# The last 24 visits of a gated attention-and-mixer kernel: score banks, one token block moved, a last sum in two halves

## The chip, the cores and the metric

The kernel runs on one core of a Trainium2 chip. The metric is device time in microseconds (us). The kernel before takes 1671.52 us in the median of three runs (1671.33 to 1672.03). The engines are TensorE (PE; its weight loads are listed as PEld), VectorE (DVE), ScalarE (ACT), GpSimd (POOL) and SyncE (SP), which here only issues DMAs.

## The reference

`x` has 2048 tokens of 640 features. Two branches are mixed by a gate for each token:

```python
g = sigmoid((x * gate_w).sum(-1, keepdims=True))
# branch A: 32 query heads of 20 features share one key and one value head
q = (x @ wq), k = x @ wk, v = x @ wv
p = softmax(q k^T * 20 ** -0.5)
a = (p v, heads side by side) @ wo
# branch B: an MLP over the token axis, 2048 -> 1728 -> 2048
b = (w2 gelu(w1 layernorm(x)^T + b1) + b2)^T
out = g * a + (1 - g) * b
```

All is float32. Products that go through the faster float32r format are split into a high and a low part, and three products (high x high, low x high, high x low) are summed; so each such step has three matmuls.

## The kernel before, in words

**Units and visits.** Attention is cut into 32 units: four blocks of 512 queries times eight groups of four heads. A unit has 16 visits, one for each block of 128 keys, 512 visits in all. A visit has four score matmuls (`qk`, L657; two use rows 0 to 63 of the array, two use rows 64 to 127, so that a pair runs side by side on the two row halves), four exponentials on ScalarE (L660) that turn a score bank in PSUM into a tile `p`, and eight matmuls of `p` with V (`pv_mm`, L684) into the bank `o`. The maximum that the softmax subtracts is found one unit ahead by other score matmuls and a reduction on DVE (L479, L482), stored (`store_max`) and fetched as two extra rows of the queries (`fetch_max`). After the last visit of a unit a chain of steps in `later` (turn, scale, back, high, low, L699 to L728) transposes `o`, divides by the sum, transposes back and splits into `oh` and `ol`, which go to `o_scr` in DRAM.

**Stretches.** Everything else is filled in beside the visits. `ph` lists 326 stretches; each is a set of fill matmuls on one row half, run beside score and maximum matmuls on the other, and carries one or two visits in turn (488 in all). The fill is first the mixer's first product, then its second (`b2_jobs`: one of 16 token blocks for each `st`, in ten stretches when `st < FIVE` and in twelve otherwise, ending on ScalarE at L758, result to `y_scr`), then the product with `wo` for the first `NA` token blocks (`a_jobs`: four stretches each, two results at L888, output at L892). `FIVE` is worked out from `NA` so that there are 326 stretches.

**The tail.** The last 24 visits run in twelve blocks of two (`for n in BLOCKS`, L1072). There are no maxima any more. Each block issues eight score matmuls, four a half, always one visit ahead of the V matmuls (`ends`, L1073; the first block issues nine, the last four), mixes them with fill matmuls of the remaining token blocks (`tail_take`, `tail_job`, L831, an accumulator for each half and each half of the 640 output features, taken up by DVE at L838), and ends with the V matmuls of two visits. Constants X_US, F_US and EXP_US spread the scores over the fill when the program is written; on the chip the order is fixed and TensorE's queue is strictly in order. PSUM has eight banks: three for maxima and fill (`ps_m`), one for fill (`ps_g`), three for scores (`ps_s`) and `o`. The last four token blocks (12 to 15) need heads of the last unit, so their product with `wo` is parted by rows of `wo`: rows 0 to 383 and 384 to 559 as fill, rows 560 to 639 last. For blocks 12 and 13 the middle part is held until after the last visit (L1115); then the last part follows for all four (L1130), DVE, ScalarE and POOL add the parts (L1133, L1136, L1137), and eight output pieces of 128 x 320 go out on the queues of SP and ScalarE (L1142).

**Loads.** `tail_load` brings the transposed heads of a token block and its `y_scr` rows from DRAM into rooms of two large tiles; the first six loads are issued from the last stretches, the rest after visit 502, all on SP.

Of the kernel before, what the change touches and what calls it, by code (L numbers as in the profile page):

```python
# [17 lines left out]
P = 128  # L18
# [14 lines left out]
NA = 10  # L33
# [6 lines left out]
def mix_kernel(ctx: ExitStack, tc: tile.TileContext, A_x, A_wq, A_wk, A_wv, A_wo,  # L40
# [595 lines left out]
    turn_p = [0]  # L636

# [12 lines left out]
    def qk(u, pr, b):  # L650
        n, kb = units[u]
        assert n in back_in
        if kb == 4 and pr == 0 and b == 0:
            new_q(n + 1)
        q = qtiles[n]
        s = ps_s.tile([P, NB], F32, name="s") if spare[0] else next_bank()
        nc.tensor.matmul(s, kst[64 * b:64 * b + 62, kb * P:(kb + 1) * P], q[64 * b:64 * b + 62, pr, :],  # L657
                         start=True, stop=True)
        p = next_p()
        nc.scalar.activation(p, s, AF.Exp, scale=SCALE)  # L660
        ptiles[u, 2 * pr + b] = p
# [12 lines left out]
    osplit = []  # L674
# [3 lines left out]
    def pv_mm(u):  # L678
# [7 lines left out]
        if kb == NS - 1:  # L686
# [27 lines left out]
            def high():  # L714
                osplit[:] = [oh, ol]
                if n < NU - 1:
                    nc.gpsimd.tensor_copy(oh, on)
                else:
                    nc.scalar.activation(oh, on, AF.Copy)

            def low():
                (nc.vector if n == NU - 1 else nc.gpsimd).tensor_sub(ol, on, f32(oh))
                for j, t in enumerate((oh, ol) if n < NU - 1 else ()):
# [70 lines left out]
    CUT = 3 * P  # L794
# [3 lines left out]
    held = (NS - 4, NS - 3)  # L798

    def room(i):  # L800
        t, at = (u0, slot[0])[i % 8 // 4], 3 * D * (i % 4)
        return (t[:, at:at + 2 * D].rearrange("p (j c q) -> p j c q", j=2, q=P), f32(t[:, at + 2 * D:at + 3 * D]))

    def tail_load(i):
        if i < len(jobs):
            st, r0, r1 = jobs[i]
            cols = slice(st * P, (st + 1) * P)
            oT, yt = room(i)
            c0, c1 = r0 // P, r1 // P
            for j in range(2):  # L810
                nc.sync.dma_start(out=f32(oT[:, j, c0:c1]),
                                  in_=o_scr[j, r0:c1 * P, cols].rearrange("(c p) s -> p c s", p=P))
                if r1 > c1 * P:
                    nc.sync.dma_start(out=f32(oT[:r1 - c1 * P, j, c1]), in_=o_scr[j, c1 * P:r1, cols])
            if r0 == 0:
                nc.sync.dma_start(out=yt, in_=y_scr[cols, :])
            loaded.append(i)

    def tail_job(n):
# [5 lines left out]
        def mm(c, k, d, h, first, last):  # L825
            if first:
                acc[d, h] = (ps_g.tile([P, NB], F32, name="g") if h and not d
                             else ps_m.tile([P, NB], F32, name="ms"))
# [3 lines left out]
            if last:  # L832
                sl = slice(d * HD2, (d + 1) * HD2)
# [166 lines left out]
    for i, (st, r0, _) in enumerate(jobs):  # L1000
        if not (r0 and st in held):
            tail_job(i)
# [68 lines left out]

    for n in BLOCKS:  # L1072
# [28 lines left out]
        waiting = {j for h in range(2) for j, _ in tail[h]}  # L1101
        while len(loaded) < len(jobs) and len(loaded) - 8 not in waiting and v >= 501:
            tail_load(len(loaded))
    accs = {}

    for c in range(CUT // P, DC):
        r = min(P, HEAD - c * P)
        for st in held:
            oT, _ = room(len(jobs) - 4 + st - (NS - 4))
            for d in range(2):  # L1110
                if (st, d) not in accs:
                    accs[st, d] = (ps_g.tile([P, NB], F32, name="g") if (st, d) == (held[1], 1)
                                   else ps_m.tile([P, NB], F32, name="ms"))
                for k, (j, w) in enumerate(((0, wo_hi), (1, wo_hi), (0, wo_lo))):
                    nc.tensor.matmul(accs[st, d][:, :HD2], oT[:r, j, c, :], w[:r, c, d * HD2:(d + 1) * HD2],  # L1115
                                     start=(k == 0 and c == CUT // P), stop=False)
    assert not tail[0] and not tail[1]
    for _, f in later[1:]:
        f()
    oh, ol = osplit  # L1120
    ends = {}
    for i in range(4):
        st = NS - 4 + i
        for d in range(2):
            at = pp_pool.tile([P, NB], F32, name="p")
            sl = slice(d * HD2, (d + 1) * HD2)
            acc = accs.get((st, d)) or (ps_s.tile([P, NB], F32, name="s") if (i, d) != (3, 1)
                                        else ps_m.tile([P, NB], F32, name="ms"))
            for k, (o, w) in enumerate(((oh, w_last[0]), (ol, w_last[0]), (oh, w_last[1]))):
                nc.tensor.matmul(acc[:, :HD2], o[:, i * P:(i + 1) * P], w[:, sl],  # L1130
                                 start=(k == 0 and (st, d) not in accs), stop=(k == 2))
            if (i, d) in ((0, 0), (1, 0), (2, 1), (3, 0), (3, 1)):
# [6 lines left out]
    for q, order in ((nc.sync, ((0, 0), (1, 0), (0, 1), (2, 1), (1, 1), (2, 0))), (nc.scalar, ((3, 0), (3, 1)))):  # L1139
# [24 lines left out]
```

## Time and profile before

| | us |
|---|---|
| median of three runs | 1671.52 |
| the profiled execution | 1671.47 |
| its span, first to last instruction | 1669.7 |
| granted TensorE clock | 1.000 |

A page of the profile gives the busy time of each engine. The timeline gives one line for a run of like instructions: start and length in us from the start of the span, the engine, the line in the kernel, output and inputs, shapes, how many, and in brackets the idle time before it with the instruction that ended it. The windows view gives, for a stretch of time, its length, then busy time and number of instructions of PE, PEld, DVE, ACT and POOL, the granted clock, the busy share of the DMA engines and GB/s. A group line with a source line gives shortest/median/longest duration in ns and the first and last start. Matmuls overlap in these records: one lasts longer than the distance to the next. The chain of work that ended last is given on the page as 95% PE, 2% issue and 1% DVE over the whole span; in the last 40 us the view puts it down to issue, and there the timelines of the engines are read instead.

### The profile page before, as it was taken

To read this page: it belongs to the slowest core of one execution; us is meant where nothing else is said; L and a number is where in the kernel's file an instruction comes from. 1 tells how busy PE (TensorE), PEld (TensorE's weight loads), DVE (VectorE), ACT (ScalarE), POOL (GpSimd) and SP (SyncE) were. 2 spreads that over 40 slices of the span, in tenths; PEclk is the share of its full clock that TensorE was granted. 3 is DMA by queue.
4 is the path that set the end of the run, shared out by engine and by line. 5 is a ranking of instruction groups with operands and counts; after the bars stand their busy time and mean duration, and the time that the engine had idled before them with its cause. 6 is when DMAs were issued, how large, how long until landed. Compare 5 with 4: busy or idle time off the path is not lost.

```text
span 1669.7 us, 38827 instructions
## 1 busy us (share of the span) xinstructions
PE 1661.0 (99%) x14865; PEld 1105.5 (66%) x14865; DVE 1435.7 (86%) x2732; ACT 1188.0 (71%) x2346; POOL 606.3 (36%) x759
## 2 busy tenths in 40 slices
PE   9999999999999999999999999999999999999998
PEld 7899666666666666666666666666666566666665
DVE  6689899999989999988888988988888998988933
ACT  4434777777777777777777777777777777777775
POOL 6578555455455554422232332122122220111210
PEclk9999999999999999999999999999999999999999
DMA  7665222222132232222222222212222121333611
GB/s 211 205 176 137 79 71 69 78 58 78 53 84 73 71 82 74 58 60 62 66 75 74 55 62 66 61 52 71 63 66 60 55 65 41 96 111 113 189 51 39
DMA packets 178305, 138.20 MB, mean 83 GB/s; under 512 B 33306, under 2 KB 144055, under 8 KB 178119
## 3 DMA queue, kind: packets, MB, share of 16 engines
q1 hardware_dynamic: 177830, 135.39, 28.9%
q8 instruction: 117, 1.92, 0.5%
q14 instruction: 70, 0.57, 0.1%
q10 hardware_dynamic: 288, 0.33, 0.1%
HBM read 102.36 MB, written 31.65 MB: 80 GB/s over the span
## 4 chain that ended last, share of the span: by engine, by line
PE 95%; issue 2%; DVE 1%; SPq 1%; ACT 0%; DMA 0%; POOL 0%; POOLq 0%; DVEq 0%; ACTq 0%
PE o L684 28%; PE ms L479 18%; PE s L657 13%; PE g L750 10%; PE g L929 7%; PE ms L657 5%; PE pp L298 4%; PE s L479 3%; PE pu L586 3%; PE g L875 2%; DVE mp L482 1%; PE ms L831 0%; ACT p L660 0%; PE pt L290 0%; SPq L195 0%
## 5 line engine op out<-in xcount | busy, mean ns | idle before, releaser
L482 DVE TENSOR_REDUCE mp<-ms 128x1 f32<-128x512 f32 x1514 | 967.2, 685 | 130.2 <-PE ms L479 102.7
L660 ACT ACTIVATE p<-s 128x512 f32<-128x512 f32 x1512 | 820.6, 606 | 299.4 <-PE s L657 280.2
L479 PE MATMUL ms<-kst,qmx 60*128 60x512 f32 x1514 | 646.5, 433 | 1.7 <-DVE mp L482 1.7
L657 PE MATMUL s<-qst,kst 62*128 62x512 f32 x1512 | 601.6, 403 | 0.0
L684 PE MATMUL o<-p,v_sb 128*32 128x512 f32 x4096 | 511.3, 601 | 0.0
L479 PEld LDWEIGHTS ms<-kst,qmx 60*128 60x128 f32 x1514 | 279.0, 184 | 244.9 <-ACT p L660 114.7
L482 DVE TENSOR_REDUCE mp<-s 128x1 f32<-128x512 f32 x534 | 355.6, 683 | 12.0 <-PE s L479 11.8
L660 ACT ACTIVATE p<-ms 128x512 f32<-128x512 f32 x536 | 305.1, 599 | 56.8 <-PE ms L657 50.2
L657 PEld LDWEIGHTS s<-qst,kst 62*128 62x128 f32 x1512 | 278.5, 186 | 55.2 <-DVE flag L670 31.0
L929 PE MATMUL g<-slot,wh 64*128 64x320 f32 x1280 | 297.5, 311 | 0.0
L129 POOL TENSOR_TENSOR wl<-wr,wh 128x512 fp32r<-128x512 f32 x176 | 228.6, 1300 | 43.8 <-PE g L750 17.3
L479 PE MATMUL s<-kst,qmx 60*128 60x512 f32 x534 | 230.8, 441 | 0.4 <-DVE yo L525 0.4
L684 PEld LDWEIGHTS o<-p,v_sb 128*32 128x32 f32 x4096 | 97.5, 108 | 185.3 <-issue 177.2
L657 PE MATMUL ms<-qst,kst 62*128 62x512 f32 x536 | 216.8, 405 | 0.0
L929 PEld LDWEIGHTS g<-slot,wh 64*128 64x128 f32 x1280 | 211.6, 184 | 2.0 <-issue 1.7
L750 PE MATMUL g<-slot,wh 64*128 64x320 f32 x864 | 202.1, 313 | 0.1
L750 PE MATMUL g<-u,wh 64*128 64x320 f32 x864 | 201.7, 312 | 0.0
L929 PE MATMUL g<-slot,wl 64*128 64x320 f32 x640 | 199.6, 312 | 0.0
L706 POOL TENSOR_TENSOR ot<-ot,rl 128x512 f32<-128x512 f32 x30 | 31.6, 1052 | 346.6 <-DVE rl L705 346.6
L128 POOL CAST wh<-wr 128x512 fp32r<-128x512 f32 x144 | 88.3, 613 | 188.0 <-PE g L750 81.5
L750 PEld LDWEIGHTS g<-slot,wh 64*128 64x128 f32 x864 | 143.5, 184 | 4.9 <-ACT yo L758 4.0
L750 PEld LDWEIGHTS g<-u,wh 64*128 64x128 f32 x864 | 143.5, 184 | 1.1 <-issue 1.1
(202 smaller groups left out, 2092.8 us busy)
## 6 DMA issues: line engine op xcount, KB each, us to landing
wr<-in_B_w_dram SPq DMA_DIRECT2D x152, 256.0 KB
qmx<-q_scr SPq DMA_DIRECT2D x192, 80.0 KB
qst<-q_scr SPq DMA_DIRECT2D x192, 80.0 KB
slot<-o_scr SPq DMA_DIRECT2D x20, 320.0 KB
y_scr<-yo SPq DMA_DIRECT2D x16, 320.0 KB
o_scr<-oh SPq DMA_DIRECT2D x124, 40.0 KB
o_scr<-ol SPq DMA_DIRECT2D x124, 40.0 KB
q_scr<-qh SPq DMA_DIRECT2D x19, 256.0 KB
```

Of the source, the lines that this page charges most:

```text
L128: nc.gpsimd.tensor_copy(wh, wr)
L129: nc.gpsimd.tensor_sub(wl, wr, f32(wh))
L298: nc.tensor.matmul(pp, w, t, start=first and n == 0, stop=not more and n == len(steps) - 1)
L479: nc.tensor.matmul(ms, qmax[n][64 * b:64 * b + 60, pr, qt * P:(qt + 1) * P], kst[64 * b:64 * b + 60, kq * NB:(kq + 1) * NB], start=True, s ...
L482: nc.vector.tensor_reduce(mtiles[n][:, c, kq:kq + 1], ms, axis=AX.X, op=ALU.max)
L586: nc.tensor.matmul(pu[r][:, :HD2], w[rows, c, :], h[rows, st, :], start=(st == 0 and k == 0), stop=(st == NS - 1 and k == 2))
L657: nc.tensor.matmul(s, kst[64 * b:64 * b + 62, kb * P:(kb + 1) * P], q[64 * b:64 * b + 62, pr, :], start=True, stop=True)
L660: nc.scalar.activation(p, s, AF.Exp, scale=SCALE)
L684: nc.tensor.matmul(o[32 * hh:32 * hh + 32, :], v_sb[:, kb, :], ptiles.pop((u, hh)), start=(kb == 0), stop=(kb == NS - 1), skip_group_check ...
L750: other_tile(half, nc.tensor.matmul(hold["p"][:, :HD2], w[r, fc % HS, :], u[d][r, fc, :], start=(hold["n"] == 1), stop=(hold["n"] == 6 * F ...
L875: other_tile(half, nc.tensor.matmul(hold["p"][:, :HD2], o[r, c, :], w[r, c, d * HD2:(d + 1) * HD2], start=(hold["n"] == 1), stop=(hold["n" ...
L929: other_tile(half, nc.tensor.matmul(hold["p"][:, :HD2], w[r, st % HS, :], h[d][r, st, :], start=(hold["n"] == 1), stop=(hold["n"] == 6 * NS)))
```

## The change

Five edits, all on the same stage but one:

- `NA` goes from 10 to 11: token block 10 is done in the stretches, and the tail's fill has one whole block instead of two. `FIVE` thereby goes from 13 to 15.
- In the tail the score matmuls go round four banks (three of `ps_s`, one of `ps_m`), and the fill's accumulators share three (`a_free`: one of `ps_g`, two of `ps_m`), a bank being handed back when its last matmul is issued.
- The last four blocks are parted at rows 480 and 560. Rows 0 to 479 are fill for all four (their rows from 384 on are loaded at the start of the tail, `late`); rows 480 to 559 are held to the end for all four, with a copy of these rows of `wo` made by four small DMAs (`load_mid`, after visit 492).
- The last unit's chain is written out after the loop, in two halves of 256 columns: transpose, reciprocal, product and transpose on DVE, `oh` on ScalarE, `ol` on DVE.
- The end is ordered held 0, 1, 2, last part of blocks 12 and 13, held 3, last part of 14 and 15; blocks 12 to 14 share out DVE and ScalarE differently, and the outputs go out in another order.

```diff
-NA = 10
+NA = 11
...
-        s = ps_s.tile([P, NB], F32, name="s") if spare[0] else next_bank()
+        if s_banks:
+            s = s_banks[s_turn[0] % 4]
+            s_turn[0] += 1
+        else:
+            s = next_bank()
...
-        if kb == NS - 1:
+        if kb == NS - 1 and n < NU - 1:
...
-    CUT = 3 * P
+    CUT = (H - 8) * DH
     HEAD = (H - 4) * DH
...
-    held = (NS - 4, NS - 3)
+    wo_mid = [t[:HEAD - CUT, 15 * D:16 * D] for t in (u0, slot[0])]
...
+    def load_mid():
+        for t, w in zip(wo_mid, (wo_hi, wo_lo)):
+            n = (DC - 1) * P - CUT
+            nc.sync.dma_start(out=f32(t[:n]), in_=f32(w[P - n:, DC - 2, :]))
+            nc.sync.dma_start(out=f32(t[n:]), in_=f32(w[:HEAD - CUT - n, DC - 1, :]))
...
             if first:
-                acc[d, h] = (ps_g.tile([P, NB], F32, name="g") if h and not d
-                             else ps_m.tile([P, NB], F32, name="ms"))
+                acc[d, h] = a_free.pop(0)
...
             if last:
+                a_free.append(acc[d, h])
...
+    s_banks.extend(ps_s.tile([P, NB], F32, name="s") for _ in range(3))
+    s_banks.append(ps_m.tile([P, NB], F32, name="ms"))
+    a_free.append(ps_g.tile([P, NB], F32, name="g"))
+    a_free.extend(ps_m.tile([P, NB], F32, name="ms") for _ in range(2))
+    assert not later
+    for i in range(4):
+        tail_load(NS - 4 - NA + i, late=True)
...
-            lanes[b].append((max(0.0, 0.55 + (i - 2) * EXP_US) if i > 2 else 0.0, s_next(b)))
+            lanes[b].append((max(0.0, 0.55 + (i - 3) * EXP_US) if i > 3 else 0.0, s_next(b)))
...
-        while len(loaded) < len(jobs) and len(loaded) - 8 not in waiting and v >= 501:
-            tail_load(len(loaded))
+        if v == 492:
+            load_mid()
+        if v >= 502 and len(loaded) < len(jobs):
+            for i in range(len(loaded), len(jobs)):
+                tail_load(i)
...
+    o = otile[0]
+    banks = s_banks + a_free + [o]
...
+    def turn(a, cut):
+        blocks, cols = slice(a * NB // 64, (a + 1) * NB // 64), slice(a * NB // 2, (a + 1) * NB // 2)
+        flat = ot[:, blocks].rearrange("p c e -> p (c e)")
+        nc.vector.transpose(flat, o[:, cols])
+        nc.vector.reciprocal(rl[:, blocks], ot[:, blocks, DH])
+        if cut is not None:
+            low(cut)
+        nc.vector.tensor_mul(ot[:, blocks], ot[:, blocks], rl[:, blocks, None].to_broadcast([P, NB // 64, 32]))
+        nc.vector.transpose(on[:, cols], flat)
+        nc.scalar.activation(oh[:, cols], on[:, cols], AF.Copy)
+
+    def low(a):
+        cols = slice(a * NB // 2, (a + 1) * NB // 2)
+        nc.vector.tensor_sub(ol[:, cols], on[:, cols], f32(oh[:, cols]))
+
+    turn(0, None)
+    turn(1, 0)
+    low(1)
+
+    def held(i):
+        oT, _ = room(len(jobs) - 4 + i)
+        for d in range(2):
+            for k, (j, w) in enumerate(((0, 0), (1, 0), (0, 1))):
+                nc.tensor.matmul(banks[2 * i + d][:, :HD2], oT[:HEAD - CUT, j, 0, :],
+                                 wo_mid[w][:, d * HD2:(d + 1) * HD2], start=(k == 0), stop=False)
...
-            if (i, d) in ((0, 0), (1, 0), (2, 1), (3, 0), (3, 1)):
+            if (i, d) in ((1, 0), (1, 1), (2, 1), (3, 0), (3, 1)):
...
+    for f, i in ((held, 0), (held, 1), (held, 2), (finish, 0), (finish, 1), (held, 3), (finish, 2), (finish, 3)):
+        f(i)
+    for q, order in ((nc.sync, ((1, 0), (0, 0), (1, 1), (0, 1), (2, 1), (2, 0))), (nc.scalar, ((3, 0), (3, 1)))):
```

More of the change, by code (lines that the diff above doesn't have):

```diff
@@ L1000, in mix_kernel @@
     for i, (st, r0, _) in enumerate(jobs):
-        if not (r0 and st in held):
+        if not r0:
             tail_job(i)
@@ L1117, in mix_kernel @@
[L1117 to L1120, printed above, removed]
+        if v == 492:
[3 more added lines that the diff above has]
+                tail_load(i)
+    assert not tail[0] and not tail[1] and not later and len(loaded) == len(jobs)
+    o = otile[0]
+    banks = s_banks + a_free + [o]
+    ot = ev.tile([P, NB // 32, 32], F32, name="ot")
+    rl = ev.tile([P, NB // 32], F32, name="rl")
@@ L1121, in mix_kernel, with finish @@
     ends = {}
-    for i in range(4):
+    def finish(i):
         st = NS - 4 + i
@@ L1126, in mix_kernel @@
             sl = slice(d * HD2, (d + 1) * HD2)
[L1127 to L1131, printed above, removed]
-            if (i, d) in ((0, 0), (1, 0), (2, 1), (3, 0), (3, 1)):
+            acc = banks[2 * i + d]
+            for k, (t, w) in enumerate(((oh, w_last[0]), (ol, w_last[0]), (oh, w_last[1]))):
+                nc.tensor.matmul(acc[:, :HD2], t[:, i * P:(i + 1) * P], w[:, sl], start=False, stop=(k == 2))
+            if (i, d) in ((1, 0), (1, 1), (2, 1), (3, 0), (3, 1)):
                 nc.vector.scalar_tensor_tensor(at[:, :HD2], acc[:, :HD2], g_col[:, st:st + 1], parts[st][:, sl],
```

59 lines of the change are left out of this document (23 added, 36 removed).

## The prediction

> **What bounds the kernel now.** I read the page first, for the share of each engine and the chain, then the last 80 us engine by engine, because the change sits there, and then the steady loop before it for the price of a stage.
>
> ```profile
> span 1669.7 us, 38827 instructions
> PE 1661.0 (99%) x14865; PEld 1105.5 (66%) x14865; DVE 1435.7 (86%) x2732; ACT 1188.0 (71%) x2346; POOL 606.3 (36%) x759
> 1591.19:1651.91 60.72, 60.72 (x538) 36.15 (x534) 15.52 (x29) 44.77 (x89) 2.58 (x6) 1.00 0.11 35
> 1651.91:1655.51 3.60, 3.39 (x40) 2.79 (x36) 2.51 (x6) 2.06 (x4) 0.00 (x0) 1.00 0.00 0
> 1655.51:1669.70 14.19, 9.70 (x66) 7.50 (x64) 7.07 (x13) 2.13 (x4) 2.58 (x3) 0.98 0.26 94
> ```
>
> TensorE counts as 99% busy, but a matmul's record lasts 0.3 to 0.6 us while its successor starts 0.15 us later, so the share hides short stops. The last 24 visits fall into three stretches of the windows view: eleven blocks of two visits (60.72 us), the twelfth block up to its attention-times-V matmuls (3.60), and the finish (14.19). What sets the length of a block is seen where ScalarE's exponentials stand beside TensorE's weight loads:
>
> ```profile
> 1591.73 4.51 ACT L660 ACTIVATE p<-s 128x512 f32<-128x512 f32 x9 [1.47 <-PE s L657]
> 1597.64 4.03 ACT L660 ACTIVATE p<-s 128x512 f32<-128x512 f32 x8 [1.40 <-PE s L657]
> 1603.07 4.03 ACT L660 ACTIVATE p<-s 128x512 f32<-128x512 f32 x8 [1.40 <-PE s L657]
> ...
> 1613.91 4.03 ACT L660 ACTIVATE p<-s 128x512 f32<-128x512 f32 x8 [1.40 <-PE s L657]
> 1619.48 4.03 ACT L660 ACTIVATE p<-s 128x512 f32<-128x512 f32 x8 [1.54 <-PE s L657]
> ```
>
> ```profile
> 1597.11 0.73 PE L657 MATMUL s<-qst,kst 62*128 62x512 f32 x3
> 1599.76 0.18 PEld L657 LDWEIGHTS s<-qst,kst 62*128 62x128 f32 x1 [0.16 <-ACT p L660]
> 1600.25 0.18 PEld L657 LDWEIGHTS s<-qst,kst 62*128 62x128 f32 x1 [0.31 <-ACT p L660]
> 1600.25 0.18 PEld L831 LDWEIGHTS ms<-slot,u 64*128 64x128 f32 x1
> 1600.68 0.16 PEld L684 LDWEIGHTS o<-p,v_sb 128*32 128x32 f32 x8 [0.24 <-issue]
> 1602.53 0.29 PEld L657 LDWEIGHTS s<-qst,kst 62*128 62x128 f32 x3 [0.84 <-ACT p L660]
> ```
>
> Each block has eight score matmuls and eight exponentials, 0.49 apart ((4.03 - 0.60 for the last) / 7). The loop closes like this. With three score banks the eighth score matmul needs the bank of the fifth. The first exponential starts 0.53 after the first score matmul (1597.11 to 1597.64), the fifth ends 4 x 0.49 + 0.59 later, 0.06 on the eighth score matmul goes (1600.25), 0.43 later the V matmuls start, 1.85 later the next block's first score matmul. 0.53 + 1.96 + 0.59 + 0.06 + 0.43 + 1.85 = 5.42, and the first exponentials stand 5.43 apart (1597.64 to 1603.07). Some steps are 5.57 (1613.91 to 1619.48): there a fill matmul follows the eighth score matmul on the same row half, 0.15 more. The first block has nine, hence 5.91. ScalarE idles 1.4 us a block, so neither it nor the fill is the limit; the wait on a score bank is.
>
> **Part 1, four score banks.** Now the eighth score matmul needs the bank of the fourth exponential, one step of 0.49 earlier. Eleven steps give 11 x 0.49 = 5.4. The V matmuls behind it need no later exponential: scores run one whole visit ahead (line 1073), so they use the first four of the block and older ones. Two things could take over. ScalarE: 8 x 0.49 = 3.92, under 4.93. TensorE: from first score matmul to the eighth there is now 0.53 + 1.47 + 0.59 + 0.06 = 2.65 us; on a row half lie four score matmuls of 0.23 (0.73 - 0.39 - 0.11 from the x3 row above: the third waits for the first on its half) and 10 to 11 fills of 0.147 instead of 12 to 13, 0.92 + 1.54 + 0.11 = 2.6 at most, of which about one fill lies behind the eighth. It fits by some 0.2. Writing out the order of issue with the new constants also removes the five endings of +0.15; five blocks end in two fills on the other half instead, some +0.06 each. That is another -0.45, less about 0.1 for accumulator waits below. Blocks 1 to 11: -5.7; bounds -5.4 (no gain from the endings) and -6.1 (-5.4 - 0.75, all of it, without any wait).
>
> **Part 2, three accumulator banks instead of four.** Fill on the two row halves needs two banks, so one is spare. If a half ends its sum just after the other, its next one must wait for the evacuation.
>
> ```profile
> 1653.82 0.54 DVE L838 SCALAR_TENSOR_TENSOR row<-g,g_col,row 128x320 f32<-128x320 f32 x1
> 1654.41 0.18 PEld L831 LDWEIGHTS g<-slot,u 64*128 64x128 f32 x1 [0.47 <-DVE row L838]
> 1658.78 0.60 PE L1115 MATMUL g<-slot,slot 128*128 128x320 f32 x3
> ```
>
> Last matmul 0.31 (the 0.60 of three is 0.31 + 2 x 0.147), 0.04 to DVE, 0.55 there, 0.05 to the weight load: 0.95 from the start of the last matmul to the next start, plus 0.11 for the exposed load, against 0.147 without a wait: 0.9 of stop, and everything behind it in TensorE's queue stops too. Whether it strikes is a matter of order. The 326 stretches leave the halves at score 976 and 979 (four and one, then six a stretch in turn), so one half begins its fill five matmuls ahead; in the order of issue the halves change sums in different blocks, or about 1 us apart, or with V matmuls between, until the lead is used up in block 10 (11 fills against 10 in every other block). Only block 12 has both changes next to each other: one stop of 0.9. That block then needs 0.11 + 2 x 0.23 + 14 x 0.147 + 0.9 + 0.09 = 3.6, against 3.60 today with 15 to 16 fills and short stops (0.47 above). Block 12: 0, bounds -0.4 (half the stop hidden) and +0.3.
>
> **Part 3, the eleventh token block in the steady loop.** The number of stretches stays 326: FIVE rises from 13 to 15, two output tiles of the mixer go from 12 stretches to 10, and 4 stretches go to the new block.
>
> ```profile
> L758 ACT ACTIVATE yo<-g,b2g,og_half x32: 633/643/654, 710.6 to 1416.5; 128x320 f32<-128x320 f32 x32
> 1261.40 0.64 ACT L758 ACTIVATE yo<-g,b2g,og_half 128x320 f32<-128x320 f32 x1
> L888 ACT ACTIVATE yo<-g,g_col x20: 543/562/587, 1425.0 to 1589.7; 128x320 f32<-128x320 f32 x20
> ```
>
> 26 of the 32 evacuations are of tiles in ten stretches, the last at 1261.40: 25 halves in 550.8, 4.41 a stretch. Six are of tiles in twelve, to 1416.5: 155.1 / 36 = 4.31. Twenty for token blocks from 1416.5 to 1589.7: 173.2 / 40 = 4.33. So 20 x 4.41 + 4 x 4.33 - 24 x 4.31 = +2.1. The 60 extra matmuls are carried by all stretches being filled a little more, and cost 2.1, not the 30 x 0.147 = 4.4 of their bare time on two halves; bounds +1.5 (the two dropped tiles at the pace of the last ones) and +3.1 (at that of the first).
>
> **Part 4, loads.** Behind the last maximum's store SP now issues eight loads (rows 384 to 480), then the fetch of that maximum; after visit 492 four small copies; after 502 eight loads where 16 were.
>
> ```profile
> 1592.28 0.34 SPq L504 DMA_DIRECT2D m_scr<-mt  x1
> 1593.73 2.74 SPq L511 DMA_DIRECT2D qst<-m_scr  x4
> 1622.38 0.34 SPq L811 DMA_DIRECT2D slot<-o_scr  x1
> 1622.83 0.37 SPq L814 DMA_DIRECT2D slot<-o_scr  x1
> ```
>
> At 0.45 each, from 1592.6, they put the fetch at 1596.2 to 1598.9 by today's clock, 7.7 us after the tail's start (today it waits 1.1 for the store and is out at 1596.5). The first score matmul that reads it belongs to visit 496, in block 4, 16 us after the start: 8 us of cover for the landing, cost 0; without that cover the excess would stand in front of block 4, on TensorE and all behind it. The rows from 384 on are first used in block 3, 10 us on: cost 0.
>
> **Part 5, the finish.** Counted from the last V matmuls (1655.51):
>
> ```profile
> 1657.36 1.58 PE L1115 MATMUL ms<-slot,slot 128*128 128x320 f32 x9
> 1657.58 0.72 DVE L700 STREAM_TRANSPOSE ot<-o 128x512 f32<-128x512 f32 x1 [0.54 <-PE o L684]
> 1658.33 0.25 DVE L705 RECIPROCAL rl<-ot 128x16 f32<-128x16 f32 x1
> 1658.62 0.69 DVE L706 TENSOR_TENSOR ot<-ot,rl 128x512 f32<-128x512 f32 x1
> 1659.41 0.71 DVE L712 STREAM_TRANSPOSE on<-ot 128x512 f32<-128x512 f32 x1
> 1660.16 0.63 ACT L719 ACTIVATE oh<-on 128x512 fp32r<-128x512 f32 x1 [5.65 <-DVE on L712]
> 1660.83 0.69 DVE L722 TENSOR_TENSOR ol<-on,oh 128x512 fp32r<-128x512 f32 x1 [0.70 <-ACT oh L719]
> 1664.90 0.31 PE L1130 MATMUL ms<-row,oh 128*128 128x320 f32 x1
> 1665.30 0.54 DVE L1133 SCALAR_TENSOR_TENSOR p<-ms,g_col,row 128x320 f32<-128x320 f32 x1
> 1665.41 0.90 ACTq L1142 DMA_DIRECT2D out_dram<-p  x2
> ...
> 1592.04 0.21 DVE L503 STREAM_TRANSPOSE mt<-mn 128x32 f32<-128x32 f32 x1 [0.97 <-POOL mn L497]
> ...
> 1666.00:1668.00 2.00, 0.00 (x0) 0.00 (x0) 0.00 (x0) 0.00 (x0) 0.00 (x0) 1.00 0.98 350
> ```
>
> 24 held and 24 last matmuls before, 24 and 24 after; only the order differs. TensorE now has 48 x 0.147 = 7.1 and its last start is at 9.39. Halves of 256 columns do not occur before; bounds are half of the whole row (0.36) and the whole row (0.72). Two transposes, 32 and 512 columns, lie on a line of 1.04 ns a column, which gives 0.44; I take that, 0.43 for the others and 0.49 on ScalarE. With today's gaps: first transpose 2.07 to 2.51, reciprocal to 2.79, product to 3.26, transpose to 3.80, oh to 4.33; meanwhile the second transpose to 4.28, reciprocal to 4.56, ol 4.60 to 5.03. TensorE has done 18 held and one last matmul at 4.75 and waits for ol until 5.18; 28 more at 0.147 put the last start at 9.30. The second half's ol is done near 7.0, ahead of its use at 7.7. So the sums end when they do now. What changes is the output. Today five of the eight pieces (160 KB, 0.47 us each at the 350 GB/s of the last row, where the engines are 98% busy) are issued between 9.4 and 10.35 and queue up; by the same walk pieces of blocks 12 and 13 go by 8.9, leaving four behind them, and the queue drains 0.4 earlier. Finish: -0.4, bounds -0.9 (halves at 0.36) and +0.4 (halves at 0.55).
>
> The Trainium skill, "DMA: Bandwidth & Descriptors", "Anatomy of one DMA", says that most of the fixed cost of a transfer is the receipt after its last byte. By that alone the end would follow the last issue, which moves 0.1, and the sum would be -3.7. The saturated window above speaks for the queue.
>
> **Sum.** -5.7 + 0 + 2.1 + 0 - 0.4 = -4.0 on the profiled execution's 1671.47 (span 1669.7 and 1.8 around it); the median of the runs, 1671.52, is the same to 0.05. Forecast 1667.5.
>
> **The rivals.**
> (a) The bank is not what holds the block: fill or ScalarE takes its place and blocks stay at 5.42. Against: a rest of 0.2 to 0.3 in TensorE's sum; for: that rest is thin. 1671.5 + 2.1 - 0.4 = 1673.2.
> (b) Whole-tile waits: the last sums of the first half wait for the second ol, at 7.1 instead of 5.1. +2.0: 1669.5. Against it:
>
> ```profile
> 1626.58 0.37 SPq L814 DMA_DIRECT2D u<-o_scr  x1
> ...
> 1626.68 0.45 PE L831 MATMUL ms<-slot,u 64*128 64x320 f32 x2
> ```
>
> A load into one part of tile u is issued while matmuls read another.
> (c) The added block costs its bare 4.4, because the pace of a stretch belongs to its place in the loop, not its form: +2.3, 1669.8.
> (d) Slower: the accumulators. If the halves end together at each of the nine changes of sums, each costs 0.9: +8.1, 1675.6. It decides from eight changes on (7.2); in today's trace only block 12 shows such a wait (0.47), and there the lead of five is gone too. The Trainium skill, "TensorEngine Tiling (Array Packing)", "Gotcha 1: PSUM Pressure", has row tiles write to different banks and so speaks against giving one away; no run here yet shows three.
>
> **How the numbers follow.** Forecast 0.70, (a) 0.08, (b) 0.08, (c) 0.09, (d) 0.05. 0.2% is 3.3 us, about what this kernel's measurement tells from none: faster means under 1668.2, slower over 1674.9. The forecast's own range is 1666.2 to 1669.0; about a tenth of the whole lies above 1668.2, so faster 0.60. (a), (b), (c) and that tenth are "same", 0.35; (d) slower, 0.05. The low ends together (-6.1 - 0.4 + 1.5 - 0.9) give 1665.6, seldom all at once; the range runs from 1666.0 to 1670.3, past (b) and (c).
>
> **What would show it.** Steps between groups of eight exponentials at 4.9 to 5.0, with the last two score waits behind the fourth; evacuation waits on TensorE only in block 12; 4.41 a stretch kept up for two more tiles; the last output matmul at 9.3 and data done earlier. Steps of 5.4, or evacuation waits in every block, would make the forecast wrong.

## The result, and the profile after

The changed kernel takes 1677.36 us in the median of seven runs (1676.00 to 1678.59), the kernel before 1672.03 on the same chip (seven runs, 1671.33 to 1672.61). The ratio is 1.0031, with a 95% interval of 1.002 to 1.0043: slower by 0.3%, against a forecast of 1667.5. The profiled execution took 1678.59.

The table cuts the profiled executions at the same places as the prediction: the steady stage runs from the first L758 on ScalarE to the last output of a token block there (L888 before, L896 after), the tail from there to the start of the last V matmuls, the finish from there to the end of the span. The last column, `e1_pad64`, is an experiment told below.

| us | before | after | after, again (`e0`) | forecast change | measured change (after; `e0`) | `e1_pad64` |
|---|---|---|---|---|---|---|
| steady stage | 879.11 | 881.18 | 881.10 | +2.1 | +2.07; +1.99 | 880.99 |
| tail | 65.82 | 71.08 | 69.46 | -5.7 | +5.26; +3.64 | 60.33 |
| finish | 14.19 | 13.41 | 13.46 | -0.4 | -0.78; -0.73 | 13.42 |

Two of the three terms came inside their bounds: the steady stage at its forecast, the finish at about twice its own. The tail missed by 11.0 in the one execution and by 9.3 in the other. (Some 0.5 of the longer span of the first lies ahead of the steady stage, which starts at 711.13 there and at 710.58 before and in `e0`.) Here are the row of busy times on the page of the kernel after, and its windows view for these three stretches and for 3.45 us inside the tail:

```profile
PE 1667.8 (99%) x14877; PEld 1109.7 (66%) x14877; DVE 1432.7 (85%) x2725; ACT 1190.0 (71%) x2349; POOL 607.9 (36%) x761
```

```profile
711.13:1592.31 881.18, 880.89 (x7990) 567.73 (x7990) 790.71 (x1501) 651.64 (x1279) 212.04 (x265) 1.00 0.27 75
1592.31:1663.39 71.08, 71.08 (x538) 38.19 (x530) 13.98 (x28) 48.54 (x95) 3.40 (x6) 0.98 0.11 32
1663.39:1676.80 13.41, 9.43 (x65) 7.46 (x64) 6.94 (x17) 2.20 (x5) 2.58 (x3) 0.94 0.27 98
1613.65:1617.10 3.45, 3.45 (x18) 0.59 (x16) 0.17 (x1) 0.60 (x1) 0.00 (x0) 0.53 0.00 0
```

PE is 99% busy as before and busy for the whole of the tail: by this column nothing stands still. The steps between the exponentials of one block and the next, on ScalarE's timeline of the kernel after, show that something does:

```profile
1599.78 1.09 ACT L665 ACTIVATE p<-s 128x512 f32<-128x512 f32 x2 [0.91 <-PE s L662]
...
1604.78 1.09 ACT L665 ACTIVATE p<-s 128x512 f32<-128x512 f32 x2 [0.98 <-PE s L662]
...
1609.72 1.09 ACT L665 ACTIVATE p<-s 128x512 f32<-128x512 f32 x2 [0.91 <-PE s L662]
...
1617.69 1.09 ACT L665 ACTIVATE p<-s 128x512 f32<-128x512 f32 x2 [3.40 <-PE s L662]
...
1622.90 1.08 ACT L665 ACTIVATE p<-s 128x512 f32<-128x512 f32 x2 [1.18 <-PE s L662]
...
1628.60 1.08 ACT L665 ACTIVATE p<-s 128x512 f32<-128x512 f32 x2 [1.42 <-PE s L662]
...
1634.82 1.09 ACT L665 ACTIVATE p<-s 128x512 f32<-128x512 f32 x2 [1.29 <-PE s L662]
```

(An exponential reads `s` or, for the fourth bank, `ms`, so a block is now several lines; those shown are the first of their blocks.) The first line is the second block's. The first two steps are 5.00 and 4.94, which is what four banks were forecast to give. Then come 7.97, 5.21, 5.70 and 6.22, and no later step is under 5.2. What the later blocks have that the first three don't is seen on TensorE's weight loads of one of them:

```profile
1628.64 0.19 PEld L838 LDWEIGHTS g<-slot,u 64*128 64x128 f32 x1
1629.01 0.18 PEld L838 LDWEIGHTS ms<-slot,u 32*128 32x128 f32 x1 [0.19 <-issue]
1629.35 0.18 PEld L838 LDWEIGHTS g<-slot,u 64*128 64x128 f32 x1 [0.16 <-issue]
1629.69 0.18 PEld L838 LDWEIGHTS ms<-slot,u 32*128 32x128 f32 x1 [0.16 <-issue]
1630.03 0.18 PEld L838 LDWEIGHTS g<-slot,u 64*128 64x128 f32 x1 [0.15 <-issue]
1630.37 0.18 PEld L838 LDWEIGHTS ms<-slot,u 32*128 32x128 f32 x1 [0.16 <-issue]
```

Six fill matmuls, three on each row half, start one after the other, 0.34 apart. Elsewhere a fill of one half and a fill of the other start together and the next pair follows 0.147 later. The loads of 32 rows are the odd ones. They come from the new cut. Rows are handed to the two halves in chunks of 128. Of rows 384 to 479 the first half gets 64 and the second half the remaining 32. That makes 4 token blocks x 2 halves of the output x 3 products = 24 matmuls of 32 rows, which the kernel before didn't have. The groups view of the kernel after, over the whole span, counts these loads and gives the idle time ahead of them, with what ended it:

```profile
L838 PEld LDWEIGHTS ms<-slot,u 32*128 32x128 f32 x18 | 3.2, 181 | 3.4 <-issue 3.4
L838 PEld LDWEIGHTS g<-slot,u 32*128 32x128 f32 x6 | 1.1, 181 | 1.2 <-issue 1.2
```

"issue" means that they waited for nothing that the profile shows: it names no bank, no accumulator and no load that was late. The view of waits, for the tail of the kernel after (total, times, longest), says the same of nearly all waits of the fills, and of eight score matmuls:

```profile
...
PEld s L662 <- ACT p L665: 7.9, 13, 0.8
PEld ms L838 <- issue: 4.7, 25, 0.3
PEld s L662 <- issue: 4.1, 8, 1.7
PEld g L838 <- issue: 2.2, 12, 0.3
...
PEld ms L838 <- DVE row L846: 0.2, 1, 0.2
```

The lines for the scores need care. The first score load of a block stands 0.84 after the last weight load of the V matmuls, in all eleven later blocks, before the change as after it (once 1.66 in the tail after, where the clock is low). The view puts this down to ScalarE in some blocks (the prediction shows one, at 1602.53) and to "issue" in others, here on the timeline of the kernel before:

```profile
1640.92 0.29 PEld L657 LDWEIGHTS s<-qst,kst 62*128 62x128 f32 x3 [0.84 <-issue]
```

In the second execution of the kernel after (`e0`), where the clock holds, the line "s <- issue" is 3.3 in eight places, three of 0.84 and five of about 0.16; each of the five comes right behind a 32-row load. Of the thirteen waits for ScalarE, 7.9 in all, eight are such 0.84; only the other five, 1.2, lie inside a block. A wait for "issue" is no sign by itself either: weight loads of V matmuls have some 36 of them, 9.6 to 10.3 in all, in the tail of every version. New after the change are those of the fills, 6.9 together.

The step of 7.97 has a second cause besides. In the last line of the windows above the granted clock is 0.53 for 3.45 us, and the V matmuls in it take nearly twice their 1.92:

```profile
1613.65 3.53 PE L688 MATMUL o<-p,v_sb 128*32 128x512 f32 x16
```

### The profile page after: what moved, and what is told of

Its sections match the earlier page's. It is cut to its first block, busy times and chain, and to the rows that moved or that the text cites. A ratio compares the mean times of both kernels' runs of the same rounds, so it can differ in the third digit from the quotient of the medians.

```text
span 1676.8 us, 38838 instructions
## 1 busy us (share of the span) xinstructions
PE 1667.8 (99%) x14877; PEld 1109.7 (66%) x14877; DVE 1432.7 (85%) x2725; ACT 1190.0 (71%) x2349; POOL 607.9 (36%) x761
## 3 DMA queue, kind: packets, MB, share of 16 engines
q8 instruction: 117, 1.92, 0.5%
## 4 chain that ended last, share of the span: by engine, by line
PE 97%; DVE 2%; SPq 1%; ACT 0%; issue 0%; DMA 0%; DVEq 0%; ACTq 0%
PE o L688 29%; PE ms L479 19%; PE s L662 14%; PE g L750 10%; PE g L937 7%; PE ms L662 4%; PE pp L298 4%; PE g L883 3%; PE s L479 2%; PE pu L586 2%; PE ms L838 1%; DVE mp L482 1%; PE g L838 1%; PE pt L290 0%; DVE yo L529 0%
## 5 line engine op out<-in xcount | busy, mean ns | idle before, releaser
L482 DVE TENSOR_REDUCE mp<-ms 128x1 f32<-128x512 f32 x1576 | 1004.6, 685 | 134.1 <-PE ms L479 106.4
L665 ACT ACTIVATE p<-s 128x512 f32<-128x512 f32 x1551 | 843.5, 605 | 319.5 <-PE s L662 306.3
L479 PE MATMUL ms<-kst,qmx 60*128 60x512 f32 x1576 | 672.9, 433 | 2.7 <-DVE mp L482 2.7
L662 PE MATMUL s<-qst,kst 62*128 62x512 f32 x1551 | 614.1, 401 | 0.1
L479 PEld LDWEIGHTS ms<-kst,qmx 60*128 60x128 f32 x1576 | 290.5, 184 | 262.4 <-ACT p L665 121.4
L482 DVE TENSOR_REDUCE mp<-s 128x1 f32<-128x512 f32 x472 | 315.9, 684 | 8.7 <-PE s L479 8.4
L662 PEld LDWEIGHTS s<-qst,kst 62*128 62x128 f32 x1551 | 286.1, 186 | 43.5 <-DVE flag L675 23.5
L665 ACT ACTIVATE p<-ms 128x512 f32<-128x512 f32 x497 | 285.8, 599 | 40.0 <-PE ms L662 37.2
L479 PE MATMUL s<-kst,qmx 60*128 60x512 f32 x472 | 207.1, 445 | 0.4 <-DVE yo L525 0.4
L662 PE MATMUL ms<-qst,kst 62*128 62x512 f32 x497 | 200.0, 402 | 0.0
```

The lines of the kernel that those rows point to most:

```text
L479: nc.tensor.matmul(ms, qmax[n][64 * b:64 * b + 60, pr, qt * P:(qt + 1) * P], kst[64 * b:64 * b + 60, kq * NB:(kq + 1) * NB], start=True, s ...
L482: nc.vector.tensor_reduce(mtiles[n][:, c, kq:kq + 1], ms, axis=AX.X, op=ALU.max)
```

## The experiments

The theory on which the runs were chosen: TensorE doesn't run a 32-row tile beside a 64-row one but empties between them, and 24 such tiles cost the tail some 9 us, while the other four parts of the change do what was forecast. Against it stood the accumulators (three where four were), the fourth bank itself, the clock, and the added block's loads. Ratios are to the kernel before on the same chip, with 95% intervals.

**The change again** (`e0_after_again`), nothing edited, to see whether the clock's drop belongs to the kernel.

> The changed kernel once more, unaltered, for a second profile. In the first profile the V matmuls of the fourth block took 3.53 us instead of 1.92 at a granted clock of 0.53. If that drop of the clock is a chance event of single executions, this execution has it in another place or not at all, and without it takes about 1676.4 (1678.59 less 1.7 to 2). If it belongs to the change, it comes back in the same block. In either case the steps between groups of eight exponentials are 4.9 to 5.0 before the first matmul with 32 rows and 5.2 to 6.4 after it.

1676.37 in the one run. The drop isn't there. The same block now takes 6.34:

```profile
1609.08 1.09 ACT L665 ACTIVATE p<-s 128x512 f32<-128x512 f32 x2 [0.91 <-PE s L662]
1615.42 1.09 ACT L665 ACTIVATE p<-s 128x512 f32<-128x512 f32 x2 [1.75 <-PE s L662]
```

So 1.6 of the 7.97 belongs to the one execution and not to the kernel, and the rest of the loss comes without it.

**The 32 rows filled up to 64 with zeros** (`e1_pad64`). GpSimd clears the unused rows of the chunk, and the second half's matmul takes all 64 rows. The number of matmuls stays the same, and zeros add nothing to a sum.

```diff
-            r = slice(64 * h, min(r1 - c * P, 64 * h + 64))
+            r = slice(64 * h, 64 * h + 64 if r1 == CUT else min(r1 - c * P, 64 * h + 64))
...
     for i in range(4):
         tail_load(NS - 4 - NA + i, late=True)
+        nc.gpsimd.memset(f32(room(NS - 4 - NA + i)[0][CUT % P:, :, CUT // P]), 0.0)
```

> The 24 matmuls of 32 rows become matmuls of 64 rows: rows 96 to 127 of the heads' tile are filled with zeros by POOL, so the sum is the same. Theory (a matmul of 32 rows cannot run beside one of 64 rows, and TensorE empties itself at each change, 0.34 us a matmul instead of 0.147 for a pair): no weight load of TensorE waits for 'issue' among the fills, all steps between groups of eight exponentials are 4.9 to 5.1, the tail up to the last V matmuls is 58.7 us, and the time is 1667.4 (1672.0 + 2.1 - 5.7 - 0.8). Rival 'three accumulator banks': steps stay at 5.2 to 6.4 and the time at 1676. Rival 'the late loads of rows 384 to 479': the same, 1676.

1667.31 (seven runs, 1666.42 to 1667.93), ratio 0.9971 [0.996, 0.9982]. The tail in its windows view, and the waits of the tail:

```profile
1591.35:1651.68 60.33, 59.72 (x537) 33.77 (x529) 13.76 (x28) 47.40 (x95) 4.46 (x10) 1.00 0.14 38
```

```profile
PEld s L662 <- ACT p L665: 12.0, 21, 0.8
...
PEld ms L838 <- DVE row L846: 1.3, 3, 0.8
```

No fill waits for "issue" any more, and the steps are 4.93 to 5.11 from the second block to the last. TensorE waits for score banks again: eleven of the 21 waits are the 0.84 at the head of a block, the other ten, 2.8, are for a bank inside a block, where `e0_after_again` has 1.2. Two of its late blocks on ScalarE's timeline, 5.01 apart:

```profile
1638.65 1.09 ACT L665 ACTIVATE p<-s 128x512 f32<-128x512 f32 x2 [0.90 <-PE s L662]
...
1643.66 1.09 ACT L665 ACTIVATE p<-s 128x512 f32<-128x512 f32 x2 [0.98 <-PE s L662]
```

What is left is the stop for an accumulator in the last block, where the prediction had put its only one:

```profile
1649.73 0.18 PEld L838 LDWEIGHTS ms<-slot,u 64*128 64x128 f32 x1 [0.76 <-DVE row L846]
```

With 64 rows everywhere the change is worth 5.0 on this chip, where the kernel before took 1672.35 (by the interval 3.0 to 6.7), and 4.0 was forecast. The 32 rows more that are read cost nothing that shows.

**Two of the four blocks filled up** (`e2_pad_two`): token blocks 12 and 13 with zeros as above, 14 and 15 left with 32 rows.

```diff
+            r = slice(64 * h, 64 * h + 64 if r1 == CUT and st < NS - 2 else min(r1 - c * P, 64 * h + 64))
...
+        if i < 2:
+            nc.gpsimd.memset(f32(room(NS - 4 - NA + i)[0][CUT % P:, :, CUT // P]), 0.0)
```

> The zeros for token blocks 12 and 13 alone; blocks 14 and 15 keep their 12 matmuls of 32 rows. Theory: steps of 4.9 to 5.1 up to the eighth, then 6.2, 6.4, 5.2 and 5.4 for the last block; tail 63.5 us; 1672.2. Rivals: 1676, or steps that do not change at the ninth.

1672.32, ratio 1.0 [0.9991, 1.0009]: 12 matmuls of 32 rows give about half the loss of 24. The steps on ScalarE's timeline are 4.9 to 5.1 from the second block until the unfilled token blocks are reached, then 6.22, 6.31 and 5.21. The lines show the last short step and the first long one:

```profile
1630.47 1.09 ACT L665 ACTIVATE p<-s 128x512 f32<-128x512 f32 x2 [0.91 <-PE s L662]
...
1635.58 1.09 ACT L665 ACTIVATE p<-s 128x512 f32<-128x512 f32 x2 [1.07 <-PE s L662]
...
1641.80 1.09 ACT L665 ACTIVATE p<-s 128x512 f32<-128x512 f32 x2 [1.33 <-PE s L662]
```

**One row more than 32** (`g1_pad33`): the same zeros, but only 33 rows are read, so that the height alone is tested.

```diff
+            r = slice(64 * h, min(64 * h + 64, CUT % P + 1 if r1 == CUT and c == CUT // P else r1 - c * P))
```

> As the run with 64 rows, but the 24 matmuls have 33 rows: the 32 real ones and one of zeros. Theory 'a matmul of up to 32 rows is set up as a 32-row tile, one of 33 to 64 rows as a 64-row tile, and TensorE empties itself between tiles of different height': no wait for 'issue' among the fills, steps of 4.9 to 5.1, 1667.3. Rival 'any matmul that does not fill its half stops the other half': steps of 5.2 to 6.4, 1676. One row more of zeros decides over 9 us.

1667.72, ratio 0.9969 [0.9960, 0.9979], not to be told from 64 rows. On the timeline of weight loads the 33-row tiles start beside the 64-row ones, and the pairs follow at 0.15; this is to be laid beside the six lines of 32-row tiles in the section on the result:

```profile
1625.93 0.19 PEld L838 LDWEIGHTS g<-slot,u 64*128 64x128 f32 x1
1625.94 0.19 PEld L838 LDWEIGHTS ms<-slot,u 33*128 33x128 f32 x1
1626.08 0.18 PEld L838 LDWEIGHTS g<-slot,u 64*128 64x128 f32 x1
1626.09 0.19 PEld L838 LDWEIGHTS ms<-slot,u 33*128 33x128 f32 x1
```

**Another cut** (`f1_cut448`): the parts are cut at row 448, so the second half has no rows at all in that chunk, and 112 rows are held to the end.

```diff
-    CUT = (H - 8) * DH
+    CUT = 448
```

> The changed kernel with the parts cut at row 448 instead of 480, nothing padded: each half of a fill has 64 rows, the 112 rows from 448 to 559 are held to the end in the same 24 matmuls. Half 0 keeps 126 fills, half 1 has 102. Theory of the 32-row matmuls: no wait for 'issue' among the fills, although no row is padded; but halves of unlike length change their sums close together more often, so there are stops for accumulators in the middle of the tail: steps of 5.1 to 5.5, tail 60.8, about 2 us over the run with 64 rows, 1669.4. Rival 'the zeros themselves help': 1676.

1669.44, ratio 0.9985 [0.9976, 0.9994]. No waits for "issue" among the fills, as expected. The waits that stand in their place are those for accumulators, four of them for the sums of `row`, 2.6 where `e1_pad64` has 1.3, and two of 0.6 together for the whole token block. The tail is 62.42, 2.1 longer than in `e1_pad64`, about what these waits have more. With the chunk on one half only, the halves end their sums at other places; that this is the cause was argued, not tried:

```profile
PEld ms L838 <- DVE row L846: 1.8, 3, 0.8
...
PEld g L838 <- DVE row L846: 0.8, 1, 0.8
```

**Three score banks again** (`g2_pad_3banks`): `e1_pad64` with three score banks and four accumulators, the scores spread as before.

```diff
-            s = s_banks[s_turn[0] % 4]
+            s = s_banks[s_turn[0] % 3]
...
-    s_banks.append(ps_m.tile([P, NB], F32, name="ms"))
...
-    a_free.extend(ps_m.tile([P, NB], F32, name="ms") for _ in range(2))
+    a_free.extend(ps_m.tile([P, NB], F32, name="ms") for _ in range(3))
...
-            lanes[b].append((max(0.0, 0.55 + (i - 3) * EXP_US) if i > 3 else 0.0, s_next(b)))
+            lanes[b].append((max(0.0, 0.55 + (i - 2) * EXP_US) if i > 2 else 0.0, s_next(b)))
```

> The run with 64 rows, with three score banks and four for accumulators, as before the change. Theory: each step between groups of eight exponentials is 5.42 again, the first 5.91, no stop for an accumulator, the last block 2.7 instead of 3.6; tail 62.9 instead of 58.7, 1671.5. Rival 'the fourth bank only uses up a rest that fewer fills had made': steps of 5.0, 1667 to 1668.

1671.48, ratio 0.9995 [0.9986, 1.0004]. The step is back at 5.42, in every block but the first, which has nine exponentials and takes 5.92:

```profile
1601.94 4.03 ACT L665 ACTIVATE p<-s 128x512 f32<-128x512 f32 x8 [1.40 <-PE s L662]
1607.36 4.03 ACT L665 ACTIVATE p<-s 128x512 f32<-128x512 f32 x8 [1.39 <-PE s L662]
```

The tail is 64.44 against 60.33 in `e1_pad64`: a fourth bank for scores, in place of a fourth accumulator, is worth 4.1 there. The intervals of the two ratios don't overlap.

**The fourth bank on the kernel before** (`e3_before_4banks`): only the banks of the tail are changed, four for scores and three for accumulators; ten token blocks, the cut at row 384 and the finish stay as they were.

```diff
+        if s_banks:
+            s = s_banks[s_turn[0] % 4]
+            s_turn[0] += 1
...
+                acc[d, h] = a_free.pop(0)
...
+    s_banks.extend(ps_s.tile([P, NB], F32, name="s") for _ in range(3))
+    s_banks.append(ps_m.tile([P, NB], F32, name="ms"))
+    a_free.append(ps_g.tile([P, NB], F32, name="g"))
+    a_free.extend(ps_m.tile([P, NB], F32, name="ms") for _ in range(2))
...
-            lanes[b].append((max(0.0, 0.55 + (i - 2) * EXP_US) if i > 2 else 0.0, s_next(b)))
+            lanes[b].append((max(0.0, 0.55 + (i - 3) * EXP_US) if i > 3 else 0.0, s_next(b)))
```

> The kernel before with one part of the change alone: four banks for scores and three for the fill's accumulators in the tail; one more whole token block is left in the tail (12 to 13 fills a half and block instead of 10 to 11) and the parts are cut at 384 rows. Theory (the wait on a score bank sets 5.42; three accumulators cost a stop where both halves change together): steps of 5.0 to 5.65, tail 62.9 against 64.3, 1670.5. Rival 'the bank is not what holds the block': steps stay at 5.42 and 5.57, 1672. Rival 'all of the bank's 0.49 comes': steps of 4.95, 1666.5.

1670.88, ratio 0.9992 [0.9983, 1.0001]: no difference that can be told from none at this interval. Its steps are 5.0 to 5.8, and its waits show why:

```profile
PEld ms L835 <- DVE row L843: 2.1, 5, 0.8
PEld g L835 <- DVE row L843: 1.0, 2, 0.7
...
PEld ms L835 <- DVE yo L843: 0.7, 2, 0.5
```

With two whole blocks of fill in the tail, three accumulators stop TensorE for 3.8 in nine places, where the kernel before has one stop of 0.5. The tail of this one profile is 64.95 against 65.82. So with two blocks of fill the fourth bank brings little, if anything, and most of its worth comes together with the block moved out of the tail.

**The eleventh block back in the tail** (`g4_pad_na10`): `e1_pad64` with

```diff
-NA = 11
+NA = 10
```

> The run with 64 rows, with NA = 10: the whole token block stays in the tail, FIVE is 13 again. Theory: the steady loop gives back 2.1 (its last result lands where it did before the change), and the tail needs 61.0 instead of 58.7, since 13 fills a half no longer fit beside four score banks in the later blocks: 1667.5, the same as with NA = 11 within the scatter. Rival 'the tail has the room': 1665.2. Rival 'each moved fill costs its bare time': 1669.6.

1670.07, ratio 0.9984 [0.9975, 0.9992], 2.6 more than expected. Times on this chip run higher (the kernel before takes 1673.01 here), and by the ratios it is some 2.2 above `e1_pad64`, with intervals that overlap. Its windows view for the tail, and two rows of its waits:

```profile
1590.85:1654.09 63.24, 62.16 (x598) 38.35 (x590) 15.99 (x32) 47.40 (x95) 4.47 (x10) 1.00 0.15 42
```

```profile
PEld g L838 <- DVE row L846: 1.5, 3, 0.8
PEld ms L838 <- DVE row L846: 1.0, 2, 0.6
```

The stages, against `e1_pad64`: steady 879.58 instead of 880.99 (-1.4, where the block's price was put at 2.1), tail 63.24 instead of 60.33 (+2.9: 60 more matmuls, and stops of 2.5 for accumulators where `e1_pad64` has 1.3), finish 14.31 instead of 13.42. The last outputs are issued at the same distance from the last V matmuls in both (9.7), so the 0.9 of the finish lies in their flight; why is open, and one execution can't say whether it comes back.

**The finish in one piece** (`g3_pad_whole`): `e1_pad64` with the last unit's chain over 512 columns at once and all four held blocks ahead of the last parts.

```diff
-    turn(0, None)
-    turn(1, 0)
-    low(1)
+    flat = ot.rearrange("p c e -> p (c e)")
+    nc.vector.transpose(flat, o)
+    nc.vector.reciprocal(rl, ot[:, :, DH])
...
-    for f, i in ((held, 0), (held, 1), (held, 2), (finish, 0), (finish, 1), (held, 3), (finish, 2), (finish, 3)):
+    for f, i in ((held, 0), (held, 1), (held, 2), (held, 3), (finish, 0), (finish, 1), (finish, 2), (finish, 3)):
```

> The run with 64 rows, with the last unit's chain whole (512 columns) and all four held sums ahead of the last ones, as before the change. Theory: the last sums wait for ol, last start some 9.6 after the last V matmuls instead of 9.2, outputs later and closer together; the finish is 14.1 instead of 13.4: 1668.0. Rival 'the halves bring nothing': 1667.3.

1668.38, ratio 0.9974 [0.9965, 0.9983]. The finish is 14.2 against 13.4 in `e1_pad64`, the tail the same (60.30). The one profile gives the halves 0.8; the intervals of the ratios overlap and don't settle it.

**The last stop taken out** (`h1_pad_shift`): `e1_pad64`, with the second half's last two sums in another order, so that the halves don't end together in the last block.

```diff
+    tail[1][:] = tail[1][:15] + tail[1][30:] + tail[1][15:30]
```

> The run with 64 rows, with one move in the order: on half 1 the second sum of the whole token block comes last instead of second, so that the halves never change their sums together. Theory (the last block loses 0.9 where both halves change and only one accumulator bank is spare): the last block needs 2.7 instead of 3.6 up to its V matmuls, no stop for an accumulator is left, tail 57.8 instead of 58.7, 0.9 us under the run with 64 rows: 1666.4. Rival 'exponentials or the last loads hold the last block': 3.6 again, 1667.3.

1666.13 (five runs, 1665.83 to 1666.61), ratio 0.9966 [0.9952, 0.9979]. The tail is 59.29 instead of 60.33, the last block takes 2.72 up to its V matmuls instead of 3.62, and its view of waits has no line for an accumulator any more, only those for score banks:

```profile
PEld s L662 <- ACT p L665: 12.6, 23, 0.8
```

This version has the lowest median of the runs and is ahead of the kernel before and of the changed one. That it is ahead of `e1_pad64` rests on the profile, 1.0 in the tail; the ratios, 0.9966 and 0.9971, don't tell the two apart.

## Why the prediction was wrong

**Part 1, the step that failed.** "On a row half lie four score matmuls of 0.23 and 10 to 11 fills of 0.147 ... It fits by some 0.2." The count of the fills was right; their one price was not. A fill costs 0.147 only while its neighbour on the other half has a tile height that runs beside it. At 24 of them the neighbours take turns: 0.34 each, so 0.68 for a pair that was put at 0.147, 0.53 too little. 24 x 0.53 = 12.8. Part of it falls into time in which TensorE had waited anyway: waits put down to a score bank inside the blocks go from 3.1 in `e1_pad64` to 1.8 in `e0_after_again` (2.8 to 1.2 on `s`, 0.3 to 0.6 on `ms`), and those for accumulators from 1.3 to 0.2. That leaves 10.4, and the tails of the two differ by 9.1. The estimate runs high: it takes each of the 24 with a full pair, and some of them stand behind one another or next to a score matmul.

The prediction worked out the new cut's rows for their loads (Part 4) and for the held matmuls (Part 5), but not for the rows that each half of the array gets. Rows of the trace before bore on it. Where the held matmuls go from 128 rows to 48, the timeline of weight loads shows a stop for which nothing was late:

```profile
1659.32 0.74 PEld L1115 LDWEIGHTS ms<-slot,slot 48*128 48x128 f32 x5 [0.19 <-issue]
```

It is as long as the first stop above (0.19), and it was passed over because it happens once there. It didn't give the rule, though: the tail before also has twelve fills of 48 rows on one half beside fills of 64 rows on the other, and its groups view shows no idle time ahead of them (the last figure):

```profile
L831 PEld LDWEIGHTS ms<-slot,u 48*128 48x128 f32 x12 | 1.9, 185 | 0.0
```

So unlike heights as such were no warning, and 32 rows beside 64 didn't occur in that tail. Neither the range nor a rival allowed for it: rival (a) has another limit take the bank's place, but stops at 5.42 a block and at 1673.2, and rival (d), at 1675.6, puts the loss down to accumulators, which cost 0.2 in the tail after.

**The rest of Part 1** held. Four banks give steps of 4.93 to 5.01 wherever no 32-row tile stands (two steps of the changed kernel, all but one of 5.11 in `e1_pad64`, not counting the first blocks with their nine exponentials), against 5.42 with three (`g2_pad_3banks`). The tail of `e1_pad64` is 5.5 shorter than before, against 5.7 forecast.

**Part 2** held: in `e1_pad64` three stops of 1.3 together, the largest 0.76 in the last block (forecast: one of 0.9 there), which takes 3.62 up to its V matmuls (forecast 3.6). The other two, 0.5 together, were not forecast. Rival (d), accumulators at every change of sums, didn't come; it is a real danger, though, where the tail carries more fill (3.8 in `e3_before_4banks`). What the prediction drew on in the Trainium skill, "TensorEngine Tiling (Array Packing)", "Gotcha 1: PSUM Pressure", therefore didn't decide here: three accumulators sufficed, but for these stops.

**Part 3** held: +2.07 against +2.1, and +1.99 and +1.88 in `e0_after_again` and `e1_pad64`. Moving the block back in `g4_pad_na10` took 1.4 off the steady stage of its one profile. Rival (c), 4.4, falls.

**Part 4** held. The fetch of the last maximum is issued from 1599.07 to 1601.8 on SP's queue, as the timeline of the kernel after shows; the prediction put its end at 1598.9 on the clock of before, which is 1601.5 here, where the tail starts 2.6 later (1592.31 for 1589.69). No score or fill waits for a load in the view of waits.

```profile
1599.07 2.73 SPq L511 DMA_DIRECT2D qst<-m_scr  x4
```

**Part 5** was right in kind and too small. The timelines of the finish after, on VectorE, TensorE and ScalarE's queue:

```profile
1665.46 0.45 DVE L1135 STREAM_TRANSPOSE ot<-o 128x256 f32<-128x256 f32 x1 [1.10 <-PE o L688]
...
1666.18 0.42 DVE L1139 TENSOR_TENSOR ot<-ot,rl 128x256 f32<-128x256 f32 x1
```

```profile
1672.59 0.31 PE L1167 MATMUL o<-row,oh 128*128 128x320 f32 x1
```

```profile
1673.09 0.96 ACTq L1181 DMA_DIRECT2D out_dram<-p  x2
```

A half row takes 0.45 and 0.42 (forecast 0.44 and 0.43). The last output matmul starts 9.20 after the last V matmuls (forecast 9.30, before 9.39). The rest is the flight of the outputs: from the start of the last pair of issues to the end of the span 3.71 instead of 4.29, so -0.78 in all, against -0.4 with bounds of -0.9 and +0.4. That pair starts 9.70 after the last V matmuls instead of 9.90, so the end did not simply follow the last issue, as the prediction's other reading, -3.7 in the sum, had it. (The section of the Trainium skill that it names for this describes transfers issued by GpSimd; these go out from SP and ScalarE.) The first matmul with `ol` starts 4.98 after the last V matmuls (its weight load stands at 1668.37), where rival (b) had 7.1: (b) falls.

In `e1_pad64`, where the 24 fills are 64 rows high and all else is as changed, the three stages of the profile sum to +1.88 - 5.49 - 0.77 = -4.4, against the forecast of -4.0. The miss is that one term. That the sum comes so near is luck in part: the finish gained 0.4 more than forecast, and the tail 0.2 less.

## What to carry to other kernels

When a cut moves, write out for every piece how many rows each part of the array gets, and look for a remainder of 32: here filling it up with zero rows cost nothing that shows and turned a loss of 0.3% into a gain of 0.3%. A TensorE busy 99% doesn't say that matmuls run side by side: look at the distance from start to start, and at short "issue" waits among weight loads, which deserve a look even where they occur once. A bank, an accumulator and the amount of fill are one budget: the fourth score bank was worth 4.1 us with one block of fill fewer in the tail, and nothing that could be told from none on the kernel before.

## What was not expected of the hardware

A 32-row tile doesn't run beside a 64-row tile, though its rows are others; a 33-row tile does (`g1_pad33`), a 48-row one does (the kernel before), and so do tiles of 64 with 64. In the six lines in the section on the result each change between 32 and 64 rows costs a stop of 0.15 to 0.19, so the starts lie 0.34 apart instead of two in 0.147. Matmuls of 80 and of 128 rows follow one another without a stop in the finish after (weight loads at 1667.69 and 1667.84). The Trainium skill, "TensorEngine Tiling (Array Packing)", "Key Properties", says that changing the tiling mode, and not only the tile, drains TensorE. The stops here agree with that, if a matmul of 33 to 64 rows counts as a 64-row tile and one of 32 rows as a 32-row tile. So the rule was at hand, on the page that the prediction named for its rival (d). Why 33 rows are treated otherwise than 32 isn't shown by any run; only the times are.

In one execution of the changed kernel the granted clock was 0.53 for 3.45 us while the profile has TensorE busy throughout, and it cost 1.6. The Trainium skill, "TensorE: Matmul & The Clock Gate", "Part 1: The HAM clock gate (the "warmup" mystery)", gives half rate after at least one idle window of about 3.4 us, and full rate after a busy one of that length. Rate and length agree; but the profile has TensorE busy for the whole of the tail ahead of it, so no idle window is seen, and what set it off stays open. A second execution of the same program didn't show it.
